# Decode block of sliding-window attention and a gated MLP: part of w_up in small loads, fewer TensorE instructions, ten wide rows of wo

## The chip, the core and the metric

The kernel runs on one core of one Trainium2 chip. The metric is device microseconds of one execution on that core; lower is better. A core has TensorE (matrix products, PE in the profile, its weight loads PEld), VectorE (DVE), ScalarE (ACT), GpSimd (POOL) and SyncE (SP), which here does nothing but issue transfers. The transfers of all issuing engines run on the same 16 DMA engines.

## The reference

Two tokens (B = 2, one position each) of width 512 are normalised; an attention over the last 4096 positions of a key and value cache and a gated MLP both read the normalised token, and both results are added to the token.

```
W = 4096; rep = 4                                  # 32 query heads, 8 key heads, Dh = 128
xn = (x - mean(x)) / sqrt(var(x) + 1e-5)           # [2, 1, 512]
q = (xn @ wq) as [2, 32, 1, 128]
k, v = k_cache[:, :, -W:], v_cache[:, :, -W:]      # [2, 8, 4096, 128], repeated 4 times
p = softmax(q @ k^T * 128**-0.5)
A = (p @ v) as [2, 1, 4096] @ wo                   # wo [4096, 512]
gate, up = xn @ W_gate, xn @ W_up                  # [512, 1792]
B = (gate * (gate > 0) * up) @ W_down              # [1792, 512]
out = x + A + B
```

Everything is float32. The weights and the two cache windows are read once, 94.9 MB, and the output is 4 KB.

## The kernel before, in words

**Where the data lies.** One SBUF tile, `ring` (line 71), has four places of 32 KB per partition. `place` hands them out in turn, and every large load goes into one or two of them: wq (two places), w_gate, w_up, then for each of four steps g (a half of the key heads, r = g // 2, of one token b = g % 2) two loads of keys and two of values (`load_kv`, line 98, 4 MB each), then w_down (`load_down`), then wo in two halves of 16 rows per partition (r = 0 and r = 1, line 457 on). SP issues all of these in this order (lines 81, 95, 106, 462). A load waits until the last reader of the data that lay in its place is done; so SP runs ahead of the compute by up to a ring's length. ACT issues the small loads of x (lines 124 and 416) and the output.

**Front.** The statistics of x give xn; `xt_ps`/`xnT` (lines 208 to 215) turn it so that the 512 features lie on the partitions, in four chunks, each column repeated 16 times. Then q = xn wq in 64 passes on four column groups of the PE array (line 223), a turn of q per head (232), a spread of it by four products with `spot` (239), and 32 small copies into `qz` (248), ACT and DVE in turn. Then gate and up (line 258), the product `hh` (267), its turn by 14 products (274) and four copies into `hT` (276).

**Four attention steps** (line 394 on). In `scores` DVE turns the keys in blocks of 32 (line 291) and PE multiplies (297); `maxima`, `softmax` and `turn` make the probabilities; `values` multiplies them with v (354); `gather` masks and adds the four column groups into `oa` (363, 369); `finish` adds and scales (378, 379). After two steps, `spread_heads` (384) puts the heads' results on the partitions by eight products, and `take_heads` copies them to `oT`.

**End.** `y_ps` [128, 128] collects the result, a quarter of the 512 output columns on each 32 partitions. w_down's 14 rows, wo's 16 rows of r = 0 and the first LATE = 8 rows of r = 1 go through `slot` (line 433): one product of 512 columns per row, into `y4`, rows in turn on four column groups that run side by side. Then DVE copies `y4` to `ys` (line 471), and `quarters` (line 440) adds it to `y_ps` by four products of 128 columns with `fold`. The last eight rows of r = 1 go through `quarters` as well: four products of 128 columns each. A float32 product is two passes in the profile, each with a weight load. r = 1 comes in five transfers, cut at rows 8, 13, 15 and 15.5 (`cuts`, line 429). ACT copies `y_ps` to `yo` and sends it out (lines 475, 476).

The order of instructions on each engine is the order of the program text (`manual_schedule`); waits are put in by which bytes an instruction touches.

Of the kernel before, what the change touches and what calls it, by code (L numbers as in the profile page):

```python
# [20 lines left out]
def kernel(  # L21
# [12 lines left out]
    nc = tc.nc  # L34
# [55 lines left out]
    MQ = P * FM // Q  # L90
    assert P * FM == F
# [27 lines left out]
    x2 = const.tile([B, D], F32, name="x2")  # L119
    wqt = load_rows(wq)  # L120
    gw = load_rows(w_gate)
    uw = load_rows(w_up)
    for c0, c1 in ((0, 256), (256, 384), (384, 512)):
        nc.scalar.dma_start(x2[:, c0:c1], x[:, 0, c0:c1])
# [11 lines left out]
    ones = const.tile([1, 1], F32, name="ones")  # L136
    nc.vector.memset(ones, 1.0)
# [4 lines left out]
    nc.gpsimd.memset(hT, 0.0)  # L142
    oT = const.tile([P, R, NJ, B, 16], F32, name="oT")
    nc.gpsimd.memset(oT, 0.0)
    xsel = const.tile([B, B, 16], F32, name="xsel")
    nc.gpsimd.memset(xsel, 0.0)
    nc.gpsimd.tensor_copy(xsel[:, :, 0], ident[0:B, 0:B])
    rep = const.tile([B, 16, B], F32, name="rep")
    nc.gpsimd.tensor_copy(rep, ident[0:B, None, 0:B].to_broadcast([B, 16, B]))

    spread = const.tile([HR, P + NE], F32, name="spread")
    nc.gpsimd.memset(spread, 0.0)
    nc.gpsimd.tensor_copy(spread[:, NE - 1:NE - 1 + P:NE], ident[0:HR, 0:HR])

# [10 lines left out]
    picks = const.tile([P, NP, 2, NP, REP], F32, name="picks")  # L165
    nc.gpsimd.memset(picks, 0.0)
    for a in range(NP):
        nc.gpsimd.tensor_copy(picks[:, a, :, a, :], of_k.rearrange("p (h i) -> p h i", h=2))
# [6 lines left out]
        out=by_h, in_=ident.rearrange("p (s x b i) -> p x i s b", s=S1, x=C, b=PB), op=ALU.add, axis=AX.XY  # L175
    )
# [31 lines left out]
    xt_ps = ps_1.tile([P, KC, 32], F32, name="xt_ps", tag="misc")  # L208
    for kc in range(KC):
        nc.tensor.matmul(  # L210
            xt_ps[:, kc, :], xn.rearrange("r (p k) -> r k p", k=KC)[:, kc], rep.rearrange("r s b -> r (s b)"),
            start=True, stop=True,
        )
    xnT = work.tile([P, KC, 32], F32, name="xnT", tag="on", bufs=1)
    nc.vector.tensor_copy(xnT, xt_ps)
# [3 lines left out]
    for kc in range(KC):  # L219
        for r in range(R):  # L220
            for c in range(C):
                n = r * C + c
                nc.tensor.matmul(  # L223
                    q_ps[r][32 * c:32 * c + 32, :], xnT[:, kc, :], wqt[:, kc, n * 512:(n + 1) * 512],
                    start=(kc == 0), stop=(kc == KC - 1),
                )
    for r in range(R):
        qs = work.tile([P, 512], F32, name=f"qs{r}", tag="qs")
        (nc.vector.tensor_copy if r else nc.scalar.copy)(qs, q_ps[r])  # L229
        qt = ps_kt.tile([P, REP, C, 16, B], F32, name=f"qt{r}", tag="kt")  # L230
        for i in range(REP):
            nc.tensor.transpose(  # L232
                qt[:, i].rearrange("p c s b -> p (c s b)"), qs[:, i * P:(i + 1) * P], ident
            )
        qT = work.tile([P, B, C, REP], F32, name=f"qT{r}", tag="qT")
        nc.vector.tensor_copy(qT, qt[:, :, :, 0, :].rearrange("p i c b -> p b c i"))  # L236
        rq = ps_1.tile([P, CB, B, C, REP], F32, name=f"rq{r}", tag="misc")
        for cb in range(CB):
            nc.tensor.matmul(  # L239
                rq[:, cb].rearrange("p b c i -> p (b c i)"), spot[:, cb].rearrange("p b e -> p (b e)"),  # L240
                qT.rearrange("p b c i -> p (b c i)"), start=True, stop=True,
            )
        for b in range(B):
            for pb in range(PB):
                rows = slice(L * pb, L * pb + L)
                for a in range(NP):
                    lo = 2 * a * 16 + pb * REP
                    (nc.vector.tensor_copy if a else nc.scalar.copy)(  # L248
                        qz[rows, r * B + b, :, :, lo:lo + REP], rq[rows, :, b, a::NP, :]
                    )  # L250
# [4 lines left out]
    for h, dst, wt in ((0, g_ps, gw), (1, u_ps, uw)):  # L255
        for kc in range(KC):
            for c in range(Q):
                nc.tensor.matmul(  # L258
                    dst[32 * c:32 * c + 32, :], xnT[:, kc, :], wt[:, kc, c * MQ:(c + 1) * MQ],
                    start=(kc == 0), stop=(kc == KC - 1),  # L260
                )
    gs = work.tile([P, MQ], F32, name="gs", tag="qs")
# [8 lines left out]
    ht_ps = ps_1.tile([32, FM * Q, B], F32, name="ht_ps", tag="misc")  # L271
    firsts = ident.rearrange("p (c r) -> p c r", c=Q)[:, :, 0:B]
    for k in range(FM):
        nc.tensor.matmul(ht_ps[:, k * Q:(k + 1) * Q], hh[:, k], firsts, start=True, stop=True)  # L274
    for c in range(Q):
        nc.vector.tensor_copy(hT[32 * c:32 * c + 32, :, :, 0], ht_ps[:, c::Q])
# [7 lines left out]
    osb, os, ons, oa = {}, {}, {}, {}  # L284
# [24 lines left out]
    def maxima(g):  # L309
# [15 lines left out]
        nc.tensor.matmul(nm_ps, mb.rearrange("p s x b i -> p (s x b i)"), ones, start=True, stop=True)  # L325
# [10 lines left out]
    def turn(g, p, l):  # L336
# [5 lines left out]
        lp = ps_1.tile([HR, 1], F32, name=f"lp{g}", tag="misc")  # L342
        nc.tensor.matmul(lp, by_h.rearrange("p x i -> p (x i)"), l, start=True, stop=True)
        rls[g] = work.tile([HR, 1], F32, name=f"rl{g}", tag="rl")
# [15 lines left out]
    def gather(g, a):  # L360
# [6 lines left out]
        if a == 0:  # L367
            oa[g] = ps_1.tile([HR, 4, P], F32, name=f"oa{g}", tag="oa")
        nc.tensor.matmul(  # L369
            oa[g], picks[:, a].rearrange("p h a i -> p (h a i)"), ons[a], start=(a == 0), stop=(a == NP - 1)  # L370
        )

    def finish(g):
        r, b = divmod(g, B)
        if b == 0:
            osb[r] = const.tile([HR, B, P], F32, name=f"osb{r}")
        su = work.tile([HR, P], F32, name=f"su{g}", tag="su", bufs=1)
        nc.vector.tensor_reduce(out=su, in_=oa[g].rearrange("h u d -> h d u"), op=ALU.add, axis=AX.X)
        nc.vector.tensor_scalar(osb[r][:, b], su, rls[g], None, op0=ALU.mult)

    def spread_heads(r, pool, tag):
        op = pool.tile([P, NJ, B], F32, name=f"op{r}", tag=tag)
        for e in range(NE):
            nc.tensor.matmul(
                op, spread[:, NE - 1 - e:NE - 1 - e + P],
                osb[r][:, :, e * NJ:(e + 1) * NJ].rearrange("h b j -> h j b"),
                start=(e == 0), stop=(e == NE - 1),
            )
        return op

    def take_heads(r, op):
        nc.vector.tensor_copy(oT[:, r, :, :, 0], op)

    for g in range(NG):
# [5 lines left out]
        if g > B and g % B == 1:  # L400
            take_heads(g // B - 1, op)
# [9 lines left out]
        if g % B == 0 and g:  # L411
            op = spread_heads(g // B - 1, ps_kt, "kt")
    dw = load_down()
    xr = work.tile([B, D], F32, name="xr", tag="qs")
    for c0 in (0, D // 2):
        nc.scalar.dma_start(xr[:, c0:c0 + D // 2], x[:, 0, c0:c0 + D // 2])
# [3 lines left out]
    nc.vector.memset(y_ps, 0.0)  # L420
    for e in range(Q):
        nc.tensor.matmul(
            y_ps[32 * e:32 * e + 17, :], xsel.rearrange("p b s -> p (b s)")[:, 0:17],
# [81 lines left out]
```

## Time and profile before

| what | value |
|---|---|
| median of 3 runs | 229.6 us (229.57 to 229.81) |
| the profiled execution: its own time | 229.65 us |
| its span, first to last instruction | 227.9 us |
| read from HBM | 94.90 MB, 417 GB/s over the span |
| busy: PE / DVE / ACT / POOL | 157.6 / 100.9 / 8.6 / 6.4 us |
| granted TensorE clock, mean | 0.918 |

The times of the rows are microseconds from the first instruction. The profiled execution's own time is 1.75 us longer than its span and 0.05 us longer than the median. PE and PEld are two columns of one engine: a matrix pass and the weight load ahead of it, which overlap. In a row of the timeline the bracket names the idle time before the first instruction and what ended it. In a row of the windows the columns are the stretch, its length, the busy time of PE, PEld, DVE, ACT and POOL with the number of instructions, the granted clock, the mean busy share of the 16 DMA engines (it can read above 1 in a short stretch), and GB/s.

### The profile page before, as it was taken

To read this page: it belongs to the slowest core of one execution; us is meant where nothing else is said; L and a number is where in the kernel's file an instruction comes from. 1 tells how busy PE (TensorE), PEld (TensorE's weight loads), DVE (VectorE), ACT (ScalarE), POOL (GpSimd) and SP (SyncE) were. 2 spreads that over 40 slices of the span, in tenths; PEclk is the share of its full clock that TensorE was granted. 3 is DMA by queue.
4 is the path that set the end of the run, shared out by engine and by line. 5 is a ranking of instruction groups with operands and counts; after the bars stand their busy time and mean duration, and the time that the engine had idled before them with its cause. 6 is when DMAs were issued, how large, how long until landed. Compare 5 with 4: busy or idle time off the path is not lost.

```text
span 227.9 us, 2200 instructions
## 1 busy us (share of the span) xinstructions
PE 157.6 (69%) x952; PEld 51.6 (23%) x952; DVE 100.9 (44%) x104; ACT 8.6 (4%) x28; POOL 6.4 (3%) x24
## 2 busy tenths in 40 slices
PE   0003982970997489596758976857999785788694
PEld 0003231430221122121112311212144121224123
DVE  2022004229993312999320499922079972213000
ACT  0002012200000100000010000010000001000000
POOL 8100000000000000000000000000000000000000
PEclk9999997697699999889967999995699999999889
DMA  9899999999999999999999999999999999999991
GB/s 369 368 437 390 458 418 426 446 443 420 426 457 397 431 460 420 410 452 426 414 449 443 423 420 449 414 426 460 408 429 449 420 420 449 413 436 437 406 402 64
DMA packets 3784, 95.03 MB, mean 417 GB/s; under 512 B 430, under 2 KB 704, under 8 KB 832
## 3 DMA queue, kind: packets, MB, share of 16 engines
q1 hardware_dynamic: 3744, 94.90, 97.2%
q8 instruction: 7, 0.11, 0.2%
q10 hardware_dynamic: 32, 0.01, 0.0%
q14 instruction: 1, 0.01, 0.0%
HBM read 94.90 MB, written 0.00 MB: 417 GB/s over the span
## 4 chain that ended last, share of the span: by engine, by line
DMA 62%; DVE 16%; PE 14%; issue 7%; ACT 1%; DVEq 0%; ACTq 0%
DMA ring<-in_A_k_cache_dram 39%; DVE kT L291 13%; DMA ring<-in_A_wo_dram 13%; DMA ring<-in_A_wq_dram 10%; PE q_ps L223 4%; PE y L435 3%; PE g_ps L258 2%; PE u_ps L258 1%; PE rq L239 1%; PE y_ps L442 1%; PE qt L232 1%; DVE qz L248 1%; ACT qz L248 1%; PE ht_ps L274 0%; DVE hh L267 0%
## 5 line engine op out<-in xcount | busy, mean ns | idle before, releaser
L291 DVE STREAM_TRANSPOSE kT<-ring 128x4096 f32<-128x4096 f32 x16 | 70.1, 4421 | 10.7 <-DMA ring<-in_A_k_cache_dram 10.7
L297 PE MATMUL s<-kT,qz 128*32 128x512 f32 x256 | 59.5, 641 | 17.9 <-DVE kT L291 17.9
L354 PE MATMUL o<-ring,pt 128*32 128x512 f32 x256 | 35.5, 656 | 4.8 <-DVE rl L345 4.8
L297 PEld LDWEIGHTS s<-kT,qz 128*32 128x32 f32 x256 | 13.8, 114 | 62.5 <-issue 34.1
L363 DVE TENSOR_TENSOR on<-o,mask 128x512 f32<-128x512 f32 x8 | 5.4, 679 | 22.9 <-PE o L354 22.9
L354 PEld LDWEIGHTS o<-ring,pt 128*32 128x32 f32 x256 | 10.1, 119 | 23.4 <-issue 18.2
L210 PE MATMUL xt_ps<-rep,xn 2*128 2x32 f32 x8 | 2.0, 414 | 18.4 <-DVE xn L206 18.4
L339 PE MATMUL pp<-p,perm 128*128 128x512 f32 x16 | 10.9, 819 | 4.5 <-ACT p L333 4.5
L341 DVE STREAM_TRANSPOSE pt<-pp 128x1024 f32<-128x1024 f32 x4 | 5.0, 1250 | 14.7 <-PE pp L339 14.7
L369 PE MATMUL oa<-on,picks 128*16 128x512 f32 x16 | 8.3, 597 | 3.8 <-DVE on L363 3.8
L223 PE MATMUL q_ps<-ring,xnT 128*32 128x512 f32 x64 | 9.1, 734 | 2.3 <-DMA ring<-in_A_wq_dram 2.3
L435 PE MATMUL y<-ring,oT 128*32 128x512 f32 x48 | 7.0, 745 | 2.0 <-DMA ring<-in_A_wo_dram 2.0
L312 DVE TENSOR_REDUCE m<-s 128x1 f32<-128x512 f32 x4 | 2.8, 692 | 12.7 <-PE s L297 12.7
L333 ACT ACTIVATE p<-s,nm 128x512 f32<-128x512 f32 x4 | 2.7, 687 | 143.0 <-DVE nm L327 143.0
L189 DVE BATCH_NORM_STATS2 stats<-x 2x6 f32<-2x512 f32 x1 | 0.7, 681 | 12.5 <-DMA x<-in_A_x_dram 12.5
L236 DVE COPY qT<-qt 128x32 f32<-128x32 f32 x2 | 0.4, 191 | 13.0 <-PE qt L232 13.0
L248 DVE COPY qz<-rq 32x32 f32<-32x32 f32 x16 | 3.0, 187 | 7.1 <-ACT qz L248 7.1
L210 PEld LDWEIGHTS xt_ps<-rep,xn 2*128 2x128 f32 x8 | 1.9, 321 | 18.3 <-issue 18.3
L305 PE MATMUL idle<-pt,ident 128*128 128x512 f32 x12 | 5.9, 618 | 0.0
L471 DVE COPY ys<-y 128x512 f32<-128x512 f32 x1 | 0.7, 692 | 11.7 <-PE y L435 11.7
L339 PEld LDWEIGHTS pp<-p,perm 128*128 128x128 f32 x16 | 3.4, 235 | 7.6 <-issue 4.0
L232 PE MATMUL qt<-ident,qs 128*128 128x128 f32 x8 | 1.7, 357 | 4.4 <-DVE qs L229 4.4
(81 smaller groups left out, 76.7 us busy)
## 6 DMA issues: line engine op xcount, KB each, us to landing
ring<-in_A_k_cache_dram SPq DMA_DIRECT2D x8, 4096.0 KB
ring<-in_A_v_cache_dram SPq DMA_DIRECT2D x8, 4096.0 KB, 26.8
ring<-in_A_wo_dram SPq DMA_DIRECT2D x1, 4096.0 KB, 28.9
ring<-in_B_W_gate_dram SPq DMA_DIRECT2D x1, 3584.0 KB, 29.9
ring<-in_B_W_up_dram SPq DMA_DIRECT2D x1, 3584.0 KB, 38.0
ring<-in_B_W_down_dram SPq DMA_DIRECT2D x1, 3584.0 KB
ring<-in_A_wo_dram SPq DMA_DIRECT2D x1, 2048.0 KB
ring<-in_A_wo_dram SPq DMA_DIRECT2D x1, 1280.0 KB
```

The source lines that it names most:

```text
L223: nc.tensor.matmul(q_ps[r][32 * c:32 * c + 32, :], xnT[:, kc, :], wqt[:, kc, n * 512:(n + 1) * 512], start=(kc == 0), stop=(kc == KC - 1),)
L248: (nc.vector.tensor_copy if a else nc.scalar.copy)(qz[rows, r * B + b, :, :, lo:lo + REP], rq[rows, :, b, a::NP, :])
L258: nc.tensor.matmul(dst[32 * c:32 * c + 32, :], xnT[:, kc, :], wt[:, kc, c * MQ:(c + 1) * MQ], start=(kc == 0), stop=(kc == KC - 1),)
L291: nc.vector.transpose(kt.rearrange("p j c k h -> p (j c k h)"), kt_in[:, JH * s1 * DH:JH * (s1 + 1) * DH])
L297: nc.tensor.matmul(ss[g][lo:lo + 32, :], qz[:, g, cb, h, 16 * a:16 * a + 32], kt[:, :, cb, :, h], start=(a == 0 and cb == 0), stop=(a == N ...
L305: nc.tensor.matmul(idle, ident, pts[g][:, 2 * n:2 * n + 2].rearrange("p n j k -> p (n j k)"), start=True, stop=True)
L339: nc.tensor.matmul(pp[:, h], perm[:, h], p, start=True, stop=True)
L341: nc.vector.transpose(pts[g].rearrange("p n j k -> p j n k"), pp.rearrange("p h y -> p y h"))
L354: nc.tensor.matmul(o[32 * q:32 * q + 32, :], pts[g][:, a * S1 + s1, j:j + 4, :].rearrange("p u k -> p (u k)"), v[:, lo:lo + 512], start=(s ...
L363: nc.vector.tensor_tensor(ons[a], os[a].rearrange("p (u d) -> p u d", u=4), mask[:, :, None].to_broadcast([P, 4, P]), op=ALU.mult)
L369: nc.tensor.matmul(oa[g], picks[:, a].rearrange("p h a i -> p (h a i)"), ons[a], start=(a == 0), stop=(a == NP - 1))
L435: nc.tensor.matmul(y4[32 * t:32 * t + 32, :], lhsT.rearrange("p b s -> p (b s)"), w, start=(i < Q), stop=(i >= EARLY - Q))
```

## The change

**w_up.** The last 320 of each partition's 7168 columns (1280 bytes, 160 KB in all) no longer come with the large load. The rest, 6848 columns, comes as one transfer of 128 rows as before. The 128 ends of 1280 bytes go elsewhere: four transfers, issued by SP behind w_up, whose source has 5, 5, 3 and 3 as its outermost count, carry 20, 20, 36 and 36 of them (by the change's own words, mostly over DMA engines 0 to 2); one transfer issued by ACT carries the other 16. They land in a zeroed area behind w_up, on other partitions, in four layers (`ES`). Four further columns of xn (`xe`, turned into `xnT[:, 4:8]`) hold the matching features, and four products more complete `u_ps`; the product that would have read the 320 columns is cut to 128.

**Loads of x.** x2 comes in one transfer ahead of everything else on ACT, not three behind; xr in one transfer of eight rows, not two of two rows.

**Fewer TensorE instructions.** The spread of q is done once for both r (4 products, not 8), and `qz` is filled by 8 copies, not 32. `hh` is turned by one DVE transpose, not 14 products and four copies. `xt_ps` and `nm_ps` are transposes. `by_row`, `picks` and `oa` are widened to 128 rows, so that `finish` writes `oT` itself with three DVE instructions per step, and `spread_heads` and `take_heads` are gone. `y_ps` is begun by one product with a wider `xsel`, not by a memset and four.

**End.** LATE is 10: ten rows of r = 1 go through `slot`, six through `quarters`. The cuts are at rows 10, 13, 15 and 15.5, and the last half row is loaded by ACT, issued ahead of SP's pieces of r = 1. The last row's quarters are taken in the order 2, 3, 0, 1.

```diff
+    MX = 320
+    ES = 4
+    SMALL = []
+    at = 0
+    for e, s0, s1 in ((5, 0, 1), (3, 1, ES)):
+        for h in range(2):
+            SMALL.append((e, h, s0, s1, at))
+            at += 4 * e * (s1 - s0)
...
+    nc.scalar.dma_start(x2, x[:, 0, :])
     wqt = load_rows(wq)
     gw = load_rows(w_gate)
-    uw = load_rows(w_up)
-    for c0, c1 in ((0, 256), (256, 384), (384, 512)):
-        nc.scalar.dma_start(x2[:, c0:c1], x[:, 0, c0:c1])
+    UC = KC * F - MX
+    ut = place(UC + ES * MX)
+    nc.vector.memset(ut[:, UC:], 0.0)
+    nc.sync.dma_start(ut[:, :UC], w_up.rearrange("(p k) f -> p (k f)", p=P)[:, :UC])
+    apart = w_up.rearrange("(p k) f -> p (k f)", p=P)[:, UC:]
+    for e, h, s0, s1, p0 in SMALL:
+        src = bass.AP(
+            tensor=apart.tensor, offset=apart[p0:p0 + 1].offset,
+            ap=[[KC * F, e], [KC * F * e, 4 * (s1 - s0)], [1, MX]],
+        )
+        nc.sync.dma_start(ut[32 * h:32 * h + 4 * e, UC + s0 * MX:UC + s1 * MX], src)
+    nc.scalar.dma_start(ut[64:64 + P - at, UC:UC + MX], apart[at:P])
+    uw = ut[:, :KC * F].rearrange("p (k f) -> p k f", k=KC)
...
+    for s in range(ES):
+        nc.tensor.matmul(
+            u_ps[32 * Q - 32:32 * Q, MQ - MX:], xnT[:, KC + s, :], ut[:, UC + s * MX:UC + (s + 1) * MX],
+            start=False, stop=(s == ES - 1),
+        )
...
-    for k in range(FM):
-        nc.tensor.matmul(ht_ps[:, k * Q:(k + 1) * Q], hh[:, k], firsts, start=True, stop=True)
-    for c in range(Q):
-        nc.vector.tensor_copy(hT[32 * c:32 * c + 32, :, :, 0], ht_ps[:, c::Q])
+    nc.vector.transpose(hT.rearrange("p k b s -> p (k b s)"), hh.rearrange("p k y -> p (k y)"))
...
-    LATE = 8
-    cuts = {0: (0, NJ), 1: (0, LATE, 13, 15, NJ - 0.5, NJ)}
+    LATE = 10
+    cuts = {0: (0, NJ), 1: (0, LATE, 13, 15, NJ - 0.5)}
...
-    down(0, Q)
-    op = spread_heads(R - 1, ps_1, "misc")
-    down(Q, 2 * Q)
-    take_heads(R - 1, op)
+    down(0, 2 * Q)
...
+        if r == R - 1:
+            nc.scalar.dma_start(flat[:, int((NJ - 0.5) * D):], rows[:, int((NJ - 0.5) * D):])
         for lo, hi in zip(cuts[r], cuts[r][1:]):
             nc.sync.dma_start(flat[:, int(lo * D):int(hi * D)], rows[:, int(lo * D):int(hi * D)])
```

149 lines of the change are left out of this document (71 added, 78 removed).

## The prediction

> **What bounds the kernel now.** I read the page first, then the stretches, then the last 15 us of the timeline.
>
> ```profile
> span 227.9 us, 2200 instructions
> PE 157.6 (69%) x952; PEld 51.6 (23%) x952; DVE 100.9 (44%) x104; ACT 8.6 (4%) x28; POOL 6.4 (3%) x24
> q1 hardware_dynamic: 3744, 94.90, 97.2%
> q8 instruction: 7, 0.11, 0.2%
> ```
>
> The queue of SP's loads fills 97.2% of 16 engines' span, no compute engine more than 69%. The stretches show that nothing interrupts it:
>
> ```profile
> 22.60:60.00 37.40, 25.72 (x190) 10.26 (x192) 14.41 (x27) 3.95 (x18) 0.00 (x0) 0.83 1.01 436
> 60.00:120.00 60.00, 45.02 (x216) 12.35 (x216) 34.44 (x25) 1.56 (x4) 0.00 (x0) 0.93 1.00 428
> 120.00:180.00 60.00, 50.38 (x265) 15.13 (x257) 35.53 (x21) 0.78 (x2) 0.00 (x0) 0.89 1.01 433
> 180.00:210.00 30.00, 22.36 (x145) 7.87 (x149) 11.76 (x17) 0.78 (x2) 0.00 (x0) 1.00 1.00 429
> 210.00:222.50 12.50, 9.68 (x68) 2.21 (x65) 0.84 (x2) 0.00 (x0) 0.00 (x0) 0.86 0.96 405
> 222.50:223.00 0.50, 0.39 (x16) 0.39 (x20) 0.05 (x1) 0.00 (x0) 0.00 (x0) 1.00 0.68 246
> 223.00:223.50 0.50, 0.50 (x29) 0.50 (x21) 0.00 (x0) 0.00 (x0) 0.00 (x0) 1.00 0.40 145
> 223.50:224.00 0.50, 0.50 (x28) 0.37 (x21) 0.00 (x0) 0.00 (x0) 0.00 (x0) 1.00 0.34 117
> 224.00:224.50 0.50, 0.50 (x23) 0.50 (x20) 0.00 (x0) 0.00 (x0) 0.00 (x0) 1.00 0.02 6
> ```
>
> The DMA share, last but one, is 1.00 within a hundredth from 22.6 to 210 us. So no compute time of the middle is worth anything; bytes per DMA engine and the tail are. The last rows: at 222.5 to 223 some engines run dry, and from 223 to 224 only 0.40 x 16 = 6.4 and 0.34 x 16 = 5.4 of 16 still work. About six engines are about 1.1 us later than the rest. A cause stands in the trace: TensorE's instructions come over the same engines.
>
> ```profile
> q8 instruction: 1, 0.02, 69.2%
> ...
> q8 instruction: 6, 0.10, 0.2%
> ```
>
> The first row is the stretch 199.7 to 199.8, in which one instruction packet begins: 0.692 x 16 x 0.1 us = 1.11 us of one engine. The last is 0 to 200 us: six such packets, as many as there are late engines. Which engines they are, no row says.
>
> The tail:
>
> ```profile
> 214.69 7.03 PE L435 MATMUL y<-ring,oT 128*32 128x512 f32 x48 [2.04 <-DMA ring<-in_A_wo_dram]
> ...
> 218.97 0.12 PEld L435 LDWEIGHTS y<-ring,oT 128*32 128x32 f32 x4 [0.31 <-issue]
> 219.64 0.31 PEld L435 LDWEIGHTS y<-ring,oT 128*32 128x32 f32 x8 [0.55 <-issue]
> 220.26 0.12 PEld L435 LDWEIGHTS y<-ring,oT 128*32 128x32 f32 x4 [0.31 <-issue]
> 220.69 0.12 PEld L435 LDWEIGHTS y<-ring,oT 128*32 128x32 f32 x4 [0.31 <-issue]
> 221.86 0.69 DVE L471 COPY ys<-y 128x512 f32<-128x512 f32 x1 [11.66 <-PE y L435]
> 222.61 0.13 PEld L442 LDWEIGHTS y_ps<-ys,fold 128*17 128x17 f32 x8 [1.80 <-DVE ys L471]
> 222.73 1.10 PEld L442 LDWEIGHTS y_ps<-ring,oT 128*17 128x17 f32 x40
> ...
> 224.30 0.69 PE L442 MATMUL y_ps<-ring,oT 128*17 128x128 f32 x12
> 224.59 0.12 PEld L442 LDWEIGHTS y_ps<-ring,oT 128*17 128x17 f32 x4
> 225.04 0.27 ACT L475 COPY yo<-y_ps 128x128 f32<-128x128 f32 x1 [32.35 <-PE y_ps L442]
> ```
>
> Two chains run side by side. The transfers': the last half row's four weight loads stand apart at 224.59, when it has landed. TensorE's: 32 wide passes of wo r = 0, then 16 of r = 1; the loads came 0.43 us apart, and the one due at 219.40 came at 219.64, so rows 0 to 8 of r = 1 landed by 219.64. Then the copy ys, then 72 narrow passes, 40 of whose loads take 1.10 us, 0.0275 each. Unhindered, the 64 loads from 222.73 would end at 224.49: TensorE's chain is only about 0.2 us shorter than the transfers'.
>
> **The change, part by part.**
>
> **Front** (early x, joined rq and qz, hT by one DVE transpose, four more u products): nothing.
>
> ```profile
> 22.73 9.15 PE L223 MATMUL q_ps<-ring,xnT 128*32 128x512 f32 x64 [2.32 <-DMA ring<-in_A_wq_dram]
> L248 DVE COPY qz<-rq 32x32 f32<-32x32 f32 x16 | 3.0, 187 | 7.1 <-ACT qz L248 7.1
> L341 DVE STREAM_TRANSPOSE pt<-pp 128x1024 f32<-128x1024 f32 x4 | 5.0, 1250 | 14.7 <-PE pp L339 14.7
> ring<-in_A_v_cache_dram SPq DMA_DIRECT2D x8, 4096.0 KB, 26.8
> ```
>
> q waits for wq, not for x. Of 32 qz copies 24 go, 24 x 0.187 = 4.5 us, under a full queue: a 4 MB load takes 4.19 MB / 0.43 = 9.8 us and lands 26.8 us after its issue, so it stood some 17 us behind others. If that cover were gone the 4.5 us would be a gain, but it isn't. Costs lie under it too: the zeroing of 1280 columns (the 1024-column DVE row, 1.25 us, is the nearest; 1.6) delays only the small loads, queued behind 11 MB; the DVE turn of 448 columns is at most 1.25; four or five issues more on SP.
>
> **finish without spread_heads**: PE loses 32 passes; DVE gains two small operations per step. The last of it lies between 206 and 214.69, where PE waits 2.04 us for wo anyway: nothing.
>
> **w_up's columns.** Sixteen engines get 160 KB evenly now, 10 KB each, 0.38 us at 429/16 = 26.8 GB/s. The price of a small packet:
>
> ```profile
> DMA packets 65, 0.06 MB, mean 117 GB/s; under 512 B 8, under 2 KB 65, under 8 KB 65
> q1 hardware_dynamic: 65, 0.06, 33.7%
> ```
>
> That is 223.5 to 224: 57 packets of 1 KB took 0.337 x 8 = 2.70 us, 0.047 each; 1280 bytes take 0.047 to 0.059. If a group with count 5 or 3 lies on so many engines, engines 0 to 2 carry 4 + 4 + 12 + 12 = 32 of them, 1.5 to 1.9 us, so +1.1 to +1.5; engines 3 and 4 eight, +0.1; ACT's 16 give each engine 0.05; engines 5 to 15 lose 0.38 - 0.05 = 0.33. If 0 to 2 are among the early ones, they go from about 1.1 us ahead to level with the late ones, and the last landing is 0.33 us earlier. I take 0.33; the ends are -0.33 (all late ones beyond engine 4) and +1.5 (one late one among 0 to 2).
>
> **Small transfers.** A lone one is dear: SP waited 2.4 us for the 4 KB output. Paid in the queue by each of the four, that would be 9.6 us. But two 128 KB transfers, issued at 201.32 and within 0.85 us, land a median 22.9 later, so at 224.2 and 224.6 at the latest: behind others in a queue the price goes under, and I take none.
>
> ```profile
> SPq L500 <- DMA out_dram<-yo: 2.4, 1, 2.4
> ...
> 201.32 0.85 SPq L462 DMA_DIRECT2D ring<-in_A_wo_dram  x2
> ...
> ring<-in_A_wo_dram SPq DMA_DIRECT2D x2, 128.0 KB, 22.9
> ```
>
> The Trainium skill (DMA: Bandwidth & Descriptors, "Anatomy of one DMA" and "Rules for kernel authors") speaks against these loads: a fixed 2.0 us for each transfer beside its bytes, and mostly overhead under 64 KB; four times that would be an estimated 8 us from that page, and the trace agrees for a lone transfer alone.
>
> **Ten wide rows.** Rows 0 to 10 are now one transfer, and the half row that came last is ahead of it: 2.5 rows of 262 KB, 0.655 MB / 0.433 = 1.51 us. It lands, as TensorE sees it, at 219.64 + 1.51 - 0.33 = 220.82. TensorE's passes of r = 0 are over by then (before, the last group was due at 219.40), so it waits. Then 20 wide passes: five groups of four, the last starts at 220.82 + 4 x 0.43 = 222.54 and ends 0.59 later (the row below), at 223.13. From the end of y (214.69 + 7.03 = 221.72) to the fold's start (222.61) it is 0.89: 224.02. Then 8 fold and 48 row passes, 56 x 0.0275 = 1.54, and 0.27 for the last: 225.83. Before, y_ps ended at 224.30 + 0.69 = 224.99. Before, rows 8 and 9 arrived while the wide passes ran; now they must have landed before the first wide pass of r = 1 starts, and TensorE's chain is last, by 225.83 - 224.99 = +0.84 us.
>
> ```profile
> L435 PE MATMUL y<-ring,oT 128*32 128x512 f32 x48 | 7.0, 745 | 2.0 <-DMA ring<-in_A_wo_dram 2.0
> L435 PE MATMUL y<-ring,hT 128*32 128x512 f32 x28 | 4.5, 598 | 0.0
> L442 PE MATMUL y_ps<-ring,oT 128*17 128x128 f32 x64 | 2.2, 274 | 0.0
> ```
>
> (0.745 is a mean over half and full clock; at full clock the same form takes 0.598.) The last landing, 224.59 - 0.33, is then hidden. yo and the store follow as before.
>
> **Sum:** the profiled execution's 229.65 + 0.84 = 230.49; it stood 0.05 over the median of its runs, so **230.4**. The parts' ends: rows 0 to 8 landed after 219.40, so up to 0.24 less; the 0.33 not gained, +1.17; a late engine among the loaded, 0.33 + 1.5 more, +2.67. That is 230.2 to 232.3.
>
> **The rivals.** 0.2%, about what can be told from no change, is 0.46 us.
>
> 1. *The late engines are no longer late* (faster). Place: the landing of rows 0 to 10. For TensorE's chain to end at 224.99 as before, that must be 0.84 earlier, at 219.98: from there on the transfers' end decides again. If the six late engines lost their 1.1 us, it would be at 219.7, and the end 224.7: 229.65 - 0.3 = 229.3. For it: 164 TensorE instructions go (28 + 32 of the turn and the spread, 12 of the tail, 8, 6 and 4 elsewhere, less 8 new, each with its load). Against it: 164 of 1904 is less than one packet in seven (1904 / 7 = 272), so six of them still come before the end. The Trainium skill (Runtime: NRT & Kernel Launch, "Instruction fetch mechanics") says the same in other words: blocks of 16 KiB, 256 instructions, fetched ahead and mostly hidden; the packets here agree in size, 0.11 MB in seven, but one costs a DMA engine 1.11 us.
>
> 2. *The loaded engines end last.* If one of 0 to 2 is late already, everything from w_up on lands 1.1 to 1.5 later on it, not 0.33 earlier: 229.6 + 0.84 + 0.33 + 1.3 = 232.1; if one of the early ones is only little ahead, 230.8 to 231.2. Against it: ten engines of 16 are early.
>
> 3. *Half clock in the tail.* The granted clock was 0.50 from 214.69 to 218.10 after an idle stretch (below). TensorE now idles longer ahead of 214.7, and again before 220.8. If r = 1's passes fall into half clock, 20 wide passes cost 0.43 x 5 = 2.1 more at most: 230.9 to 232.5.
>
> ```profile
> 214.69:218.10 3.41, 3.41 (x16) 0.79 (x20) 0.00 (x0) 0.00 (x0) 0.00 (x0) 0.50 0.98 417
> ```
>
> 4. *Small transfers at the lone price.* Four times 2.4 us on engines 0 to 2, one after the other: 229.6 + 0.8 + 9.6 = 240.
>
> **How the numbers follow.** Forecast (TensorE waits for ten rows), 0.57, of which 0.10 for a somewhat smaller wait than worked out, 229.9 to 230.06; rival 1, 0.16; rival 2, 0.15; rival 3, 0.10; rival 4, 0.02. The likeliest gives 230.4. Range 229.3 to 231.3: from rival 1's value to the milder half of rivals 2 and 3. Faster by over 0.2% is below 229.14, slower above 230.06. Rival 1 lies around the first bound, a little more than half of it beyond: 0.10 faster; the rest of it with the forecast's 0.10 within, 0.16 rounded up to 0.20 for what I have not seen; the others slower: 0.70.
>
> **What would show it.** Right: in the timeline, PE idle after r = 0's passes and released by the transfer of wo at about 220.8; ys starting at about 223.3, not 221.86; no stand-apart loads of y_ps after it, so that TensorE's queue never waits for a transfer there. DMA share zero about 0.3 us earlier than 224.5, and more than six engines at work between 223 and 224. Wrong: ys at 222.4 or before (rival 1); a DMA share that stays above zero after 224.6 (rival 2); granted clock under 1 after 220 (rival 3); a hole in the DMA share behind w_up's load (rival 4).

## The result and the profile after

The changed kernel takes **231.82 us**, the median of six executions (231.49 to 233.15); the kernel before, run beside it, 229.78 (229.57 to 230.18). The ratio is 1.0102 with a 95% interval of 1.0071 to 1.0133: slower, clear of the 0.2% that the prediction takes for no change. Four executions lie between 231.49 and 231.85 and two near 233.1; the two raise the ratio, which the medians alone would put at 1.0089. The profiled execution took 231.85.

The direction and the place were forecast, the size was not: 230.4 was predicted, with 231.3 as the upper end of the range.

From the page of the changed kernel, the span, the busy times and the queues:

```profile
span 230.0 us, 2016 instructions
PE 153.3 (67%) x870; PEld 45.1 (20%) x870; DVE 101.4 (44%) x90; ACT 6.8 (3%) x16; POOL 7.5 (3%) x27
q1 hardware_dynamic: 3728, 94.75, 96.2%
q10 hardware_dynamic: 208, 0.16, 0.2%
q8 instruction: 7, 0.11, 0.2%
```

82 matrix passes and 184 instructions are gone, and it is 2.1 us longer. The instruction packets are still seven.

The stretches of the changed kernel (columns as before):

```profile
60.00:120.00 60.00, 45.40 (x210) 12.45 (x206) 34.31 (x25) 1.55 (x4) 0.00 (x0) 0.93 1.00 430
120.00:180.00 60.00, 48.80 (x247) 12.95 (x239) 35.66 (x21) 0.78 (x2) 0.00 (x0) 0.95 1.00 430
180.00:210.00 30.00, 23.55 (x140) 6.85 (x140) 12.78 (x17) 0.78 (x2) 0.00 (x0) 1.00 1.01 431
222.50:223.00 0.50, 0.50 (x12) 0.19 (x5) 0.00 (x0) 0.00 (x0) 0.00 (x0) 1.00 0.70 285
223.00:223.50 0.50, 0.50 (x9) 0.14 (x2) 0.00 (x0) 0.00 (x0) 0.00 (x0) 1.00 0.58 238
223.50:224.00 0.50, 0.50 (x4) 0.00 (x0) 0.00 (x0) 0.00 (x0) 0.00 (x0) 1.00 0.53 199
224.00:224.50 0.50, 0.30 (x2) 0.00 (x0) 0.10 (x1) 0.00 (x0) 0.00 (x0) 1.00 0.19 64
224.50:225.00 0.50, 0.00 (x0) 0.00 (x0) 0.50 (x1) 0.00 (x0) 0.00 (x0) 1.00 0.00 0
```

The middle is as full as before. In a share rounded to a hundredth a few tenths of a microsecond do not show, and some were lost there: the table of completions further down has them. At the end more engines are late: from 223 to 224 it is 0.58 x 16 = 9.3 and 0.53 x 16 = 8.5 engines that still work, where it was 6.4 and 5.4.

The timeline of the changed kernel's last 16 us:

```profile
215.33 5.18 PE L446 MATMUL y<-ring,oT 128*32 128x512 f32 x32 [4.40 <-DMA ring<-in_A_wo_dram]
221.50 0.19 PEld L446 LDWEIGHTS y<-ring,oT 128*32 128x32 f32 x8 [1.90 <-issue]
221.53 2.77 PE L446 MATMUL y<-ring,oT 128*32 128x512 f32 x20 [1.02 <-DMA ring<-in_A_wo_dram]
221.96 0.15 PEld L446 LDWEIGHTS y<-ring,oT 128*32 128x32 f32 x4 [0.28 <-issue]
222.39 0.16 PEld L446 LDWEIGHTS y<-ring,oT 128*32 128x32 f32 x4 [0.27 <-issue]
222.82 0.14 PEld L446 LDWEIGHTS y<-ring,oT 128*32 128x32 f32 x2 [0.27 <-issue]
223.25 0.14 PEld L446 LDWEIGHTS y<-ring,oT 128*32 128x32 f32 x2 [0.28 <-issue]
224.41 0.69 DVE L481 COPY ys<-y 128x512 f32<-128x512 f32 x1 [15.51 <-PE y L446]
225.15 0.13 PEld L453 LDWEIGHTS y_ps<-ys,fold 128*17 128x17 f32 x8 [1.76 <-DVE ys L481]
225.28 1.32 PEld L453 LDWEIGHTS y_ps<-ring,oT 128*17 128x17 f32 x48
225.38 1.49 PE L453 MATMUL y_ps<-ring,oT 128*17 128x128 f32 x48
226.96 0.27 ACT L485 COPY yo<-y_ps 128x128 f32<-128x128 f32 x1 [34.11 <-PE y_ps L453]
```

TensorE is done with r = 0 at 215.33 + 5.18 = 220.51 and stands still for 1.02 us, until the ten rows have landed. From there it is the last chain: 20 wide passes, the copy ys, the fold, and 48 narrow passes with no wait between them, since all that they read landed while the wide ones ran. y_ps ends at 225.38 + 1.49 = 226.87; before it was 224.99.

The changed kernel's chain of waits says the same in its last rows (start, length, what it was):

```profile
199.04 22.35 DMA ring<-in_A_wo_dram
221.39 0.14 issue
221.53 2.78 PE y L446 x20
...
224.41 0.70 DVE ys L481
225.11 0.04 issue
225.15 1.78 PE y_ps L453 x54
226.96 0.27 ACT yo L485
```

Before, the chain left the transfers at 214.69, with r = 0; now it leaves them at 221.39, with rows 0 to 10 of r = 1.

### The profile page after: what moved, and what is told of

It reads as the page before. It is cut to its first block, busy times and chain, and to the rows that moved or that the text cites. A ratio compares the mean times of both kernels' runs of the same rounds, so it can differ in the third digit from the quotient of the medians.

```text
span 230.0 us, 2016 instructions
## 1 busy us (share of the span) xinstructions
PE 153.3 (67%) x870; PEld 45.1 (20%) x870; DVE 101.4 (44%) x90; ACT 6.8 (3%) x16; POOL 7.5 (3%) x27
## 4 chain that ended last, share of the span: by engine, by line
DMA 71%; PE 10%; DVE 9%; issue 8%; ACT 0%; ACTq 0%; DVEq 0%
DMA ring<-in_A_k_cache_dram 51%; DMA ring<-in_A_wo_dram 10%; DMA ring<-in_A_wq_dram 10%; DVE kT L321 8%; PE q_ps L252 4%; PE s L327 2%; PE o L384 1%; PE y L446 1%; PE pp L369 1%; PE y_ps L453 1%; DVE pt L371 1%; DVE ys L481 0%; DVE m L342 0%; DVE mb L351 0%; ACTq L432 0%
## 5 line engine op out<-in xcount | busy, mean ns | idle before, releaser
L327 PE MATMUL s<-kT,qz 128*32 128x512 f32 x256 | 61.4, 649 | 23.6 <-DVE kT L321 23.6
L384 PE MATMUL o<-ring,pt 128*32 128x512 f32 x256 | 30.9, 626 | 4.8 <-DVE rl L375 4.8
L384 PEld LDWEIGHTS o<-ring,pt 128*32 128x32 f32 x256 | 7.8, 115 | 24.0 <-issue 18.9
L446 PE MATMUL y<-ring,oT 128*32 128x512 f32 x52 | 7.9, 724 | 5.4 <-DMA ring<-in_A_wo_dram 5.4
L399 PE MATMUL oa<-on,picks 128*128 128x512 f32 x16 | 9.0, 645 | 3.7 <-DVE on L393 3.7
L481 DVE COPY ys<-y 128x512 f32<-128x512 f32 x1 | 0.7, 692 | 15.5 <-PE y L446 15.5
L229 PE MATMUL xt_ps<-ident,xn 2*128 2x2 f32 x4 | 0.6, 252 | 8.5 <-DVE xn L225 8.5
L252 PEld LDWEIGHTS q_ps<-ring,xnT 128*32 128x32 f32 x64 | 2.5, 130 | 18.5 <-issue 18.5
L399 PEld LDWEIGHTS oa<-on,picks 128*128 128x128 f32 x16 | 2.4, 188 | 10.3 <-DVE on L393 7.5
L446 PEld LDWEIGHTS y<-ring,oT 128*32 128x32 f32 x52 | 1.9, 129 | 11.4 <-issue 6.1
L446 PE MATMUL y<-ring,hT 128*32 128x512 f32 x28 | 3.6, 596 | 0.0
```

The lines of the kernel that those rows point to most:

```text
L252: nc.tensor.matmul(q_ps[r][32 * c:32 * c + 32, :], xnT[:, kc, :], wqt[:, kc, n * 512:(n + 1) * 512], start=(kc == 0), stop=(kc == KC - 1),)
L327: nc.tensor.matmul(ss[g][lo:lo + 32, :], qz[:, g, cb, h, 16 * a:16 * a + 32], kt[:, :, cb, :, h], start=(a == 0 and cb == 0), stop=(a == N ...
L384: nc.tensor.matmul(o[32 * q:32 * q + 32, :], pts[g][:, a * S1 + s1, j:j + 4, :].rearrange("p u k -> p (u k)"), v[:, lo:lo + 512], start=(s ...
L399: nc.tensor.matmul(oa[g].rearrange("p u e j -> p u (e j)"), picks[:, a].rearrange("p h a i e -> p (h a i e)"), ons[a], start=(a == 0), sto ...
L446: nc.tensor.matmul(y4[32 * t:32 * t + 32, :], lhsT.rearrange("p b s -> p (b s)"), w, start=(i < Q), stop=(i >= EARLY - Q))
```

## The experiments

In what follows, a wide row is one that goes through `slot`, a narrow pass one of `quarters`. The main reason on trial is that the ten rows in one transfer make TensorE wait (LATE). Its rivals for the part of the loss that was not forecast: the small loads of w_up, the half row that ACT issues ahead, the clock, and something behind the output. Each experiment ran five rounds against the kernel before, in three batches: 1 to 4, 5 to 8 and 9 to 12, in which the kernel before had medians of 229.70, 229.73 and 229.83 us. Ratios carry 95% intervals, medians are of all executions, and a difference of 0.1 us across batches can be that of the batches. A time within a kernel is that of its one profiled execution. Except where it says so, the edit is to the changed kernel.

**1. Only LATE back to 8.**

```diff
-    LATE = 10
+    LATE = 8
```

> The changed kernel with LATE back at 8: eight wide rows of r = 1, cuts at 8, 13, 15 and 15.5, all else as changed. Theory W (the wide rows set the end: they wait for a transfer of ten rows, and ten rows on four column groups take three turns of two passes, not two and a half): rows 0 to 8 land at about 221.39 - 1.25 = 220.14, eight rows take two turns, ys starts near 222.5, and the end falls back on the last landing, 224.80 + 0.45 = 225.25 for y_ps where the changed kernel had 226.87: 1.6 us less, 230.2 us. Theory S (the small loads of w_up make everything land later): the tail's order costs little, so at most 0.4 less, 231.4 us.

Measured: 230.21 (230.02 to 230.75), ratio 1.0024 (1.0015 to 1.0032). In its timeline:

```profile
215.46 7.05 PE L446 MATMUL y<-ring,oT 128*32 128x512 f32 x48 [4.39 <-DMA ring<-in_A_wo_dram]
222.65 0.69 DVE L481 COPY ys<-y 128x512 f32<-128x512 f32 x1 [13.62 <-PE y L446]
225.64 0.27 ACT L485 COPY yo<-y_ps 128x128 f32<-128x128 f32 x1 [32.64 <-PE y_ps L453]
```

The 48 wide passes of both halves run as one block again, as before the change, and yo starts 1.32 us earlier. Of the 2.0 us between the medians, LATE is 1.6.

**2. Ten wide rows, but a cut at row 8 again.** This parts the wait from the work: the same 20 wide passes, the first 16 of which need only eight rows.

```diff
-    cuts = {0: (0, NJ), 1: (0, LATE, 13, 15, NJ - 0.5)}
+    cuts = {0: (0, NJ), 1: (0, 8, LATE, 13, 15, NJ - 0.5)}
```

> The changed kernel with one cut more: rows 0 to 8 and rows 8 and 9 of r = 1 as two transfers, ten wide rows as changed. Theory W: eight rows run while rows 8 and 9 are still in flight; these land at about 221.4, their two passes each end near 222.5, ys starts near 222.7 instead of 224.41, and the last landing sets the end: 1.5 us less, 230.3 us. If the number of wide rows cost by itself, not their wait, ys would start at 223.9 and the gain were 0.5. Theory S: at most 0.3 less, 231.5 us.

Measured: 230.50 (230.31 to 231.03), 1.0037 (1.0025 to 1.0049). In its timeline:

```profile
220.27 2.77 PE L446 MATMUL y<-ring,oT 128*32 128x512 f32 x20 [1.43 <-DMA ring<-in_A_wo_dram]
223.15 0.69 DVE L481 COPY ys<-y 128x512 f32<-128x512 f32 x1 [10.34 <-PE y L446]
225.69 0.27 ACT L485 COPY yo<-y_ps 128x128 f32<-128x128 f32 x1 [32.85 <-PE y_ps L453]
```

The passes start 1.26 us earlier than in the changed kernel and everything behind them moves by 1.26 to 1.27: the wait for rows 8 and 9 is 1.3 of the 2.0 us. The expectation had ys near 222.7 if only the wait counted and at 223.9 if only the number of rows did; 223.15 lies between, so the two rows cost something by themselves as well. The 20 passes take 2.77 us in both kernels, whatever they wait for. And with that wait gone, ten wide rows are still no gain: yo starts at 225.69, in experiment 1 with eight at 225.64.

**3. w_up in one load again**, LATE stays 10. The four products, `xe` and the five small loads are gone.

```diff
-    UC = KC * F - MX
-    ut = place(UC + ES * MX)
...
-        nc.sync.dma_start(ut[32 * h:32 * h + 4 * e, UC + s0 * MX:UC + s1 * MX], src)
-    nc.scalar.dma_start(ut[64:64 + P - at, UC:UC + MX], apart[at:P])
-    uw = ut[:, :KC * F].rearrange("p (k f) -> p k f", k=KC)
+    uw = load_rows(w_up)
...
-                w = MQ - MX if (h, kc, c) == (1, KC - 1, Q - 1) else MQ
+                w = MQ
```

> The changed kernel with w_up in one load again (no small loads, no zeroed area, no further columns of xn, no four products more), ten wide rows as changed. Theory W: the wait for ten rows stays; the landings move by what the small loads did, at most 0.6 us either way: 231.2 to 232.1 us. Theory S: the last engines are those with the small loads; without them rows 0 to 10 land as reckoned from the kernel before, at 221.1 instead of 221.39 or earlier, and the spread of a load's first to last engine behind w_up falls from 2.2 to about 1.3 at the first key load: 1 us or more less, 230.8 us.

Measured: 231.59 (231.41 to 233.17, two of six above 233), 1.0107 (1.0081 to 1.0133). The profiled execution took 231.48, against 231.85 of the changed kernel, and in its timeline:

```profile
221.25 2.77 PE L418 MATMUL y<-ring,oT 128*32 128x512 f32 x20 [0.86 <-DMA ring<-in_A_wo_dram]
226.68 0.27 ACT L457 COPY yo<-y_ps 128x128 f32<-128x128 f32 x1 [34.06 <-PE y_ps L425]
```

Without the small loads the ten rows are there 0.28 us *earlier*, in one profile of each kernel. The loads carry little of the loss, and they don't bring the forecast's 0.33 us.

**4. Both undone:** w_up whole and LATE = 8.

> Both undone: w_up in one load and eight wide rows; fewer TensorE instructions, the single load of x and the half row on ACT stay. Theory W: as the kernel with eight wide rows alone, 230.2 us, or 0.3 less for the last landing. Theory S: 0.5 to 1 us below that one. What is left over the kernel before, 229.8, is neither the wide rows' nor the small loads': if it is over 230.2, the start (the first load lands 0.45 later on its last engine than before) or the waits at the end have a price of their own.

Measured: 230.19 (230.10 to 230.32), 1.0022 (1.0012 to 1.0031). Still 0.2% over the kernel before, with nothing of the two main edits left. r = 0 starts at 215.24, against 214.69: something delays the transfers ahead of r = 1 (experiments 6 and 7).

**5. The kernel before, with LATE = 10 alone.**

```diff
-    LATE = 8
+    LATE = 10
```

> The kernel before with LATE set to 10 and nothing else: ten wide rows, cuts at 10, 13, 15, 15.5 and 16, the half row still last on SP. Theory W (the wide rows set the end): rows 0 to 10 land two rows later than rows 0 to 8 did, near 220.8; three turns take 2.77 as in the changed kernel, to 223.65; ys and fold 0.85, the narrow passes 1.72: y_ps ends near 226.2 where it ended at 225.0, so 1.2 more, 230.9 us. If the waits of the other edits are needed for the loss: 229.7 to 230.0 us.

Measured: 231.00 (230.96 to 231.03), 1.0057 (1.0044 to 1.0070), +1.3 us by this one figure. In its timeline:

```profile
220.99 2.77 PE L435 MATMUL y<-ring,oT 128*32 128x512 f32 x20 [1.97 <-DMA ring<-in_A_wo_dram]
223.87 0.69 DVE L471 COPY ys<-y 128x512 f32<-128x512 f32 x1 [10.73 <-PE y L435]
226.41 0.27 ACT L475 COPY yo<-y_ps 128x128 f32<-128x128 f32 x1 [33.42 <-PE y_ps L442]
```

Here the half row still comes last, so the ten rows need two rows of 262 KB more than eight: 219.64 + 0.524 / 0.433 = 220.85, and they are seen at 220.99. The prediction's way of finding the landing holds within 0.14 us; its 2.31 us for the 20 passes doesn't.

**6. Experiment 4 with the half row last, from SP.**

```diff
-    cuts = {0: (0, NJ), 1: (0, LATE, 13, 15, NJ - 0.5)}
+    cuts = {0: (0, NJ), 1: (0, LATE, 13, 15, NJ - 0.5, NJ)}
...
-        if r == R - 1:
-            nc.scalar.dma_start(flat[:, int((NJ - 0.5) * D):], rows[:, int((NJ - 0.5) * D):])
```

> w_up in one load and eight wide rows, as the run that undid both, and the last half row again the last transfer on SP instead of ahead on ACT. Theory H (the half row ahead delays wo's first half, with which TensorE's last chain starts): r = 0 lands 0.3 to 0.4 earlier, y_ps ends 0.2 to 0.4 earlier, 229.9 us. Without it: 230.2 us. The waits of SP behind the output's landing (0.13 to 0.19 us more than before) stay in both cases.

Measured: 229.92 (229.81 to 230.17), 1.0010 (1.0002 to 1.0019): 0.27 us under experiment 4. r = 0 starts at 214.87, not 215.24, and the last load stands apart again, as in the kernel before:

```profile
221.91 0.69 DVE L451 COPY ys<-y 128x512 f32<-128x512 f32 x1 [11.66 <-PE y L418]
224.77 0.13 PEld L425 LDWEIGHTS y_ps<-ring,oT 128*17 128x17 f32 x8 [0.29 <-DMA ring<-in_A_wo_dram]
225.25 0.27 ACT L455 COPY yo<-y_ps 128x128 f32<-128x128 f32 x1 [32.44 <-PE y_ps L425]
```

**7. The kernel before, with the half row ahead on ACT:** the reverse of the edit of 6.

> The kernel before with the half row alone moved to ACT, ahead of SP's pieces of r = 1, eight wide rows. Theory H: wo's r = 0 lands 0.35 later and with it the chain of TensorE, which was 0.2 shorter than the transfers': 0.15 to 0.35 more, 229.85 to 230.05 us. Without it: 229.7 us.

Measured: 229.89 (229.81 to 230.13), 1.0009 (1.0001 to 1.0018). r = 0 starts at 215.09, 0.40 later than before, and ys at 222.28, 0.42 later. 128 KB at 0.433 MB per us are 0.30 us: the half row goes ahead of r = 0 as well, not only of r = 1, and TensorE's chain, which has become the last one, pays it.

**8. Experiment 6 with r = 0 in two transfers of eight rows,** to let TensorE begin sooner.

```diff
-    cuts = {0: (0, NJ), 1: (0, LATE, 13, 15, NJ - 0.5, NJ)}
+    cuts = {0: (0, NJ // 2, NJ), 1: (0, LATE, 13, 15, NJ - 0.5, NJ)}
```

> As the run with the half row last (w_up whole, eight wide rows), and r = 0 of wo in two transfers of eight rows, so that TensorE starts its last chain about 4.8 us earlier. Theory: TensorE's chain then has 2 us to spare and y_ps ends 0.45 after the last landing, near 225.0: 229.6 to 229.9 us, of which 0.1 to 0.2 are the waits of SP at the end. If the loss left over the kernel before lies in the landings and not in TensorE's chain: as the run without this cut, 229.9 to 230.2.

A miss: 231.29, from 229.91 to 233.19 in twelve executions, 1.0067 (1.0038 to 1.0096). The profiled one took 231.16. Its timeline, and one stretch:

```profile
219.91 3.41 PE L418 MATMUL y<-ring,oT 128*32 128x512 f32 x16 [3.06 <-DMA ring<-in_A_wo_dram]
223.46 0.69 DVE L451 COPY ys<-y 128x512 f32<-128x512 f32 x1 [13.45 <-PE y L418]
226.44 0.27 ACT L455 COPY yo<-y_ps 128x128 f32<-128x128 f32 x1 [34.07 <-PE y_ps L425]
```

```profile
219.91:223.32 3.41, 3.40 (x16) 0.65 (x16) 0.00 (x0) 0.00 (x0) 0.00 (x0) 0.55 0.84 335
```

TensorE was through with r = 0 too soon, stood still for 3.06 us, and the 16 passes of r = 1 then took 3.41 us at a granted clock of 0.55, where the same 16 take 1.92 in experiment 11. The clock fell before the passes began: in the trace it is 1.00 up to 219.55 and 0.50 from there to 222.97, and TensorE's last pass had ended at 216.85, 2.70 us earlier. This is the prediction's third rival, half clock in r = 1's passes, made by another edit. In the changed kernel's profiled execution the wait is 1.02 us, and the granted clock in the stretches from 222.5 on is 1.00. The Trainium skill (TensorE: Matmul & The Clock Gate, "What's actually happening") gives an idle window of about 3.4 us as what brings the half clock, in windows that run free of the kernel; here 2.70 us of idling sufficed. Windows of that kind would fit the spread of these twelve executions; that is argued, not shown.

**9. Experiment 6 with x in as many transfers as before** (x2 in three, still behind w_up; xr in two): 32 transfers in all, like the kernel before, not 29.

```diff
-    nc.scalar.dma_start(x2, x[:, 0, :])
...
+    for c0, c1 in ((0, 256), (256, 384), (384, 512)):
+        nc.scalar.dma_start(x2[:, c0:c1], x[:, 0, c0:c1])
...
-    nc.scalar.dma_start(xr, x[:, 0, :].rearrange("b (e f) -> (b e) f", e=Q))
+    for b in range(B):
+        nc.scalar.dma_start(xr[Q * b:Q * b + Q, :], x[b, 0, :].rearrange("(e f) -> e f", e=Q))
```

> As the run with the half row last (w_up whole, eight wide rows), and x loaded in three pieces behind w_up on ACT and xr in two transfers, so that the kernel issues 32 transfers like the one before, not 29. Theory E (what is left over the kernel before are SP's waits after the output has landed: three more semaphores, 0.06 us each, because the output's transfer is not the last in their rotation): 0.19 less than 229.92, 229.73 us. If the early x costs something in the first loads, up to 0.3 less. If neither, 229.9.

Measured: 229.82 (229.66 to 229.94), 1.0001 (0.9992 to 1.0010): no loss is left that could be told from none. Its interval overlaps that of experiment 6, so the profile has to say where the difference lies: yo starts at 225.20, only 0.05 earlier, and the rest is behind the output. Time from the end of yo to the end of the span, worked out from the traces to 0.01 us (the pages round the span to 0.1):

```
32 transfers:  before 2.56   LATE 10 alone (5) 2.56   half row ahead (7) 2.58   this one 2.56
29 transfers:  experiments 3, 4, 6    2.76  2.76  2.75
30 transfers:  experiment 8           2.68
34 transfers:  changed kernel 2.74   experiments 1, 10, 11, 12   2.73  2.74  2.75  2.73
35 transfers:  experiment 2           2.78
```

At the end SP waits for the semaphores (counters that a transfer raises when it has landed) on which the transfers count; in the trace eight of them are handed out in turn. In the trace of before, the output lands at 227.03 and the wait for it, taken at 227.05, is the last; in the changed kernel the output lands at 228.96 and three waits are taken after it, at 229.02, 229.08 and 229.14. Each costs 0.06 us. With 32 transfers the output's own comes last in the row.

**10. The changed kernel with LATE = 8 and the half row last:** the small loads of w_up stay, as the only one of the three edits.

> The changed kernel with eight wide rows and the half row last on SP, the small loads of w_up kept: the small loads in a tail that waits for nothing but the last landing. By the prediction's term for the small loads (every late engine 0.33 earlier) 0.3 less than the same kernel with w_up whole: 229.6 us. Theory S (the three loaded engines are now the last ones): 0 to 0.3 more, 229.9 to 230.2 us.

Measured: 230.12 (229.84 to 230.49), 1.0015 (1.0006 to 1.0024). Experiment 6, the same without the small loads, has 229.92: 0.20 us less, of which 0.10 lies between the two batches' medians of the kernel before. So the loads cost 0.1 to 0.2 us here, with intervals that overlap; what they don't do is gain 0.3.

**11. The same with 160 columns in place of 320.**

```diff
-    MX = 320
+    MX = 160
```

> As the last one with 160 columns in the small loads instead of 320. The three engines get half the extra, some 0.65 us, and are no longer the last; the others gain 0.16. Theory S: 0.1 to 0.3 less than with 320 columns, 229.7 to 229.9 us. By the prediction's term: 0.16 more than with 320 columns.

Measured: 229.80 (229.67 to 230.01), 1.0000 (0.9991 to 1.0008). In its timeline:

```profile
219.60 1.92 PE L446 MATMUL y<-ring,oT 128*32 128x512 f32 x16 [1.35 <-DMA ring<-in_A_wo_dram]
221.65 0.69 DVE L479 COPY ys<-y 128x512 f32<-128x512 f32 x1 [10.40 <-PE y L446]
224.51 0.13 PEld L453 LDWEIGHTS y_ps<-ring,oT 128*17 128x17 f32 x8 [0.31 <-DMA ring<-in_A_wo_dram]
224.99 0.27 ACT L483 COPY yo<-y_ps 128x128 f32<-128x128 f32 x1 [32.44 <-PE y_ps L453]
```

Half the columns, 0.32 us less, and yo starts 0.05 before the kernel before's 225.04. The end waits (2.75, not 2.56) then take that back. With 320 columns the three loaded engines end last; with 160 they are a little ahead of the late ones (the section on the prediction shows it).

**12. The changed kernel with a few idle products** on TensorE between r = 0 and r = 1, against a half clock there. They are work beside the computation, nothing of which is left out.

```diff
         if r == 0:
             down(2 * Q, FM)
+        else:
+            keep_busy(NG - 1)
```

> The changed kernel with two products of 512 columns whose result nobody reads, between TensorE's rows of r = 0 and r = 1, where it waits for ten rows. Theory W: the median stays, 231.8 us, as they fit into the wait of about 1 us or lengthen it by at most 0.2. Theory C (the executions of the changed kernel near 233.1 us are those in which the clock is halved after this wait): none near 233.1 any more, a spread under 0.6 us. If the wait has nothing to do with them: again about one execution in three near 233.1.

Measured: 232.42 (231.86 to 232.97), 1.0114 (1.0099 to 1.0129), a median 0.6 us above the changed kernel's. In its timeline:

```profile
220.40 1.98 PE L335 MATMUL idle<-pt,ident 128*128 128x512 f32 x4
222.31 2.77 PE L446 MATMUL y<-ring,oT 128*32 128x512 f32 x20
227.75 0.27 ACT L487 COPY yo<-y_ps 128x128 f32<-128x128 f32 x1 [34.93 <-PE y_ps L453]
```

The four passes take 1.98 us, the hole that they were to fill is 1.02; the ten rows wait for them, and yo starts 0.79 later than in the changed kernel. Both theories missed: the median was to stay at 231.8, and the spread, 231.86 to 232.97, is 1.1 us, not under 0.6. All five executions are moved and the highest comes close to 233.1, so the run says nothing certain on those.

## Why the prediction was wrong in its size

**Right: what decides.** "TensorE waits for ten rows" is what happens: PE is released by the transfer, ys follows from it, no narrow pass waits for a transfer, and TensorE's chain ends the kernel. Experiments 1, 2 and 5 show it from three sides. The front, `finish` without `spread_heads` and the missing TensorE instructions were costed at nothing and are worth nothing: experiment 9, which keeps them with the old tail, w_up whole and x loaded as before, can't be told from the kernel before. The early x is in experiment 6, 0.19 us over the kernel before, about what the waits at the end account for.

**The step that failed for certain: "five groups of four".** 20 passes over four column groups were taken as five starts 0.43 apart, and the last pass 0.59 long: 2.31 us. They took 2.77, in the changed kernel and in experiments 2, 3, 5 and 12. The timeline of after shows why: weight loads of four at 221.96 and 222.39, but of two at 222.82 and 223.25. Rows go to the four column groups in turn, and each row is two passes. Slots 30 to 39 give two of the groups three rows and two of them two rows. In the trace the 20 passes start in four fours and two twos, at 221.53, 221.96, 222.39, 222.81, 223.24 and 223.67: as if two passes of one group never ran side by side. That is six starts, 5 x 0.43 + 0.59 = 2.74. Eight rows are four starts, 3 x 0.43 + 0.59 = 1.88, and the 16 passes take 1.92 in experiment 11. So rows 8 and 9 cost two starts, not one, and +0.46 us was missing. By this count eleven or twelve rows would cost TensorE no more; no run tried them.

**The largest term, and a slip in its working: w_up's 320 columns, -0.33.** The landing came at 221.53 as TensorE sees it, against the 220.82 of the sum: 0.71 later. Of this, 0.33 is the gain that didn't come, 0.28 is a loss in its place (experiment 3, without the small loads, has 221.25; one profile each), and 0.10 is left for the way of working it out.

The prediction's own numbers don't give the gain. They send the loaded engines 1.1 to 1.5 us back, from 1.1 ahead of the late ones: that is 0 to 0.4 behind the place where the late ones stood *before*. The late ones then move 0.33 forward, but the loaded ones don't, and they are the last. "Level with the late ones, and the last landing is 0.33 us earlier" should have been: 0 to 0.4 later. When each of the 16 engines ended its part of a transfer shows it; this is worked out from the completions in the trace (first and last engine in us, and how many came more than 1.0 us behind the first):

```
                     w_up                first keys            last of wo
before               39.08 - 39.59   0   48.80 - 50.62   1     222.74 - 224.55    7
changed              38.80 - 39.69   0   48.68 - 50.87   4     222.60 - 224.80   10
exp. 3 (w_up whole)                                            222.71 - 224.56    7
exp. 6                                                         222.65 - 224.73    7
exp. 10                                                        222.81 - 224.80   10
exp. 11 (160)                                                  222.67 - 224.47    9
```

The price of a packet was right. Of the four small transfers of SP, the last two have 12 packets for each of three engines; their completions are 40.29, 40.41 and 40.48, then 40.96, 41.07 and 41.14, so 0.66 to 0.67 for 12 packets, 0.056 each, within the 0.047 to 0.059 of the prediction. 32 of them are 1.8 us, less the 0.38 of their share of w_up: 1.4 back, or 0.3 behind the late ones' old place.

And the three engines stay last. The first keys end last at 50.68, 50.80 and 50.87, each 9.72 or 9.73 us, the time of one load of keys, behind the last small transfer's three completions. They are 2.00 to 2.19 behind the first engine; the late ones of before are 1.2 to 1.8 behind at the end. With 160 columns the last small transfer completes at 39.92, 40.10 and 40.16; the first keys then end at 49.64, 49.81 and 49.87 on three engines and last of all, at 50.18, on another. The end of wo moves by 0.07 to 0.25 us with the small loads (experiment 10 against 6; changed kernel against experiment 3 and before), and by 0.33 back with half the columns. This is the second rival, "the loaded engines end last", in its mild form, and by another way than it was told: none of engines 0 to 2 needs to be late already, as early ones are sent further back than the late ones are. Its sign, a DMA share above zero after 224.6, did not come, nor did the forecast's, a share of zero 0.3 us sooner: from 224 to 224.5 it is 0.19, where it was 0.02.

**Not seen: behind the output.** From the end of y_ps to the profiled execution's end it was 229.65 - 224.99 = 4.66 us and is now 231.85 - 226.87 = 4.98. "yo and the store follow as before" missed 0.32 us, 0.18 of it SP's end waits; 0.04 lies between y_ps and yo and 0.10 outside the span, and no row says what made them.

**The sum.** 0.71 for the landing, 0.46 for the sixth start, 0.32 behind, less 0.13, by which the copy, the fold and the narrow passes were shorter than worked out (224.30 to 226.87 is 2.57; the prediction had 223.13 to 225.83, 2.70): 1.36, and 230.49 + 1.36 = 231.85, the profiled execution. The parts' own ends, 230.2 to 232.3, held it; the range was cut to 231.3.

**The other rivals.** Late engines no longer late: no, there are ten. The lone price for small transfers: no; all five cost 0.1 to 0.2 us (experiment 10 against 6), not 9.6. (The section of the Trainium skill that the prediction names for a fixed 2.0 us, DMA: Bandwidth & Descriptors, "Anatomy of one DMA", is on transfers that GpSimd issues; SP and ACT issue these.) Half clock in the tail: not in r = 1's passes of the profiled execution. Whether it is behind the executions near 233.1 (two of six here, two of six in experiment 3, and none above 231.1 in experiments 1, 2, 4 to 7 and 9 to 11) was not shown: there is no profile of one, and their mean granted clocks, 0.911 to 0.934, are no other than those of the rest (0.911 to 0.933). Experiment 8 shows only that a longer wait at that place can bring it. One way would fit: in the changed kernel's profile the clock is halved from 215.06 to 218.48, and r = 0's 32 passes take 5.18 us; where they run at full clock, as in experiment 9, they take 3.64. TensorE would then be done near 218.97 and wait 2.56 us, about as long as the 2.70 after which the clock fell in experiment 8, and the 1.3 us between the two sorts of executions is near the 3.41 - 1.92 = 1.49 that half clock cost there. That is argued, not shown.

## What to carry to other kernels

Before moving rows from a late chain to a wider product, ask when the *last* of them lands, and cut the transfer where the first product can start: a cut at row 8 gave back 1.3 of 2.0 us here. Count work over column groups by the fullest group, not by the mean: two rows more on four groups cost two starts here, not one. Where some engines are late and others are made later, place them all on one scale before saying which ends last. Where two chains end within a few tenths of each other, what is put ahead of one can make it the last: half a row ahead of r = 0 cost 0.16 us in experiment 7.

## What the runs showed of the hardware

- **Late engines come one by one, each behind an instruction packet.** In the trace of before such packets begin at 43.75, 65.42, 93.55 (of q14, half the size), 98.41, 129.95, 169.79 and 199.75 us. The engines more than 1.0 us behind the first of their transfer are none for w_up (39.08), then one from 48.80 on, two from 68.21, three from 97.36, four from 107.07, five from 136.22, six from 175.04 and seven from 203.01: one more behind each packet, and none catches up. So there were seven late engines, not the prediction's six. The changed kernel has the same seven steps on top of its three loaded engines: ten. No run took a packet away.
- **Small loads sit on few engines.** The four transfers of SP report 5, 5, 3 and 3 completions, the large ones 16. The Trainium skill (DMA: Bandwidth & Descriptors, "Why a DMA increments its semaphore by 16 and not by 1") says that a transfer takes the largest number of engines, up to 16, that divides the outermost counts of both sides, and the lowest-numbered ones; the trace agrees with the numbers 5 and 3. No row says which numbers the engines have.
- **Half clock after 2.70 us** of idling (experiment 8): 16 passes in 3.41 us, not 1.92.
- **The number of transfers costs at the end:** 0.06 us for each semaphore wait that SP takes after the output's landing, 0.12 to 0.22 us between 32 transfers and 29, 30, 34 or 35.
